# A convolution by Fourier transforms: the last tile's first 13 frequencies go through DRAM, ordered by frequency row, instead of being transposed on chip

## The chip, the cores and the metric

The kernel runs on one NeuronCore of one Trainium2 chip. Its engines are TensorE (PE; its weight loads are listed apart as PEld), VectorE (DVE), ScalarE (ACT), GpSimd (POOL) and SyncE (SP), which here only issues DMAs. The metric is the device time of one execution in microseconds (us); less is better. A profiled execution gives the instructions of each engine with start and duration, the DMA packets, and the TensorE clock that was granted.

## The reference

A 2D circular convolution of one 224 x 224 image with 96 channels by a 7 x 7 kernel with 96 x 96 channels, done by FFT in float32:

```python
"x": (1, 224, 224, 96) bfloat16        "w": (7, 7, 96, 96) bfloat16

wp = jnp.pad(w, ((0, H - K), (0, W - K), (0, 0), (0, 0)))
Xf = rfft2(x.astype(float32), axes=(1, 2))
Wf = rfft2(wp.astype(float32), axes=(0, 1))
Yf = jnp.einsum('bhwi,hwio->bhwo', Xf, Wf)
y = irfft2(Yf, s=(H, W), axes=(1, 2)).astype(bfloat16)
```

## The kernel before

The image's rows are cut into 8 blocks (`NJ`) of 28 output rows (`B`); with the 6 rows of overlap a block has 34 rows (`L`). Along the rows the kernel uses a short transform, along the columns taps. The columns are cut into 7 tiles (`NT`) of 32 columns: 16 pairs (`TW`) of two. The last tile is `TL` = 6.

Per tile there are three stages. **Forward**: matmuls with `Fm` turn the rows of a block into `NS` = 17 frequencies, each with two parts (frequencies 0 and 16 have two real rows each). **Middle**, `b_round(t, s, ...)`, once per tile and frequency: 33 matmuls of 96 columns (22 for frequencies 0 and 16) of the transformed pixels `xf` and their sums `J` with the transformed weights `WF`. A part of the results is copied out of PSUM by ScalarE (`tt_`), VectorE forms `u` and `v`, and the sum `ysum` of the two is the result of one frequency: 128 partitions (16 pairs x 8 blocks, "(w j)") by 384 values (2 parts r, 2 pixels m, 96 channels o). `ysum` runs on VectorE in the rounds in which `b_round` is called with `ydve` true, else on GpSimd after the round's `J` sums. **Inverse**: for a block, 34 values (17 frequencies x 2 parts) become 28 output rows. This needs the frequencies on the partitions, whereas the middle stage leaves the pixels there.

Tiles 0 to 5 turn the data through DRAM: three frequencies at a time (`YGRP`) go into `yf` and from there by one DMA to the scratch tensor `scr`; when a tile is finished, `queue_c` loads it back as `tt` with the frequencies on partitions (pieces of 384 B), and `c_jobs` inverts it during the next tile. The five loads of a tile are `LT`; one of them is made of four DMAs, two of which load 34 partitions each. `pump` issues a load when a buffer is free.

The last tile has no next tile to hide this behind. Before, its results stay on chip: `b_round` writes frequencies 0 to 12 (`SA` = 13) into `YA`, a part of the pixel buffer `xn_all`, and 13 to 16 into `YB`. VectorE turns them in squares of 32 x 32: `turn_a` four times for `YA`, during the rounds 13 to 16, and `turn_b` for `YB` behind the loop. `TA` and `TB` are the turned data. The tail then inverts: `first(j, h)` multiplies `TA` by the matrix `GA` (112 columns: 4 pixel groups x 28 rows; 384 moving columns), `second` adds four matmuls of 96 moving columns for `TB` with `GB`, and evicts the sum to `yo`. There are 16 of these pairs, 8 `first` ahead of the others. Eight output DMAs of 168 KB follow, on SyncE (4), GpSimd (3) and ScalarE (1). `GA` and `GB` come from `G` by `g_parts`: small DMAs to `GX`, then copies to `GY`, done in tiles 3 and 4.

The order of work is written by hand. The instructions of one engine stand in program order. Fills between the two halves of a round (`mid`, `fills`, `pace`) spread the inverse jobs of the tile before: `CQ[t]` = (old, new) tells how many jobs left over from two tiles ago and how many of the last tile's 11 jobs go into tile t; what is left of tile 5's jobs runs behind the loop, before the tail. All DMAs but four of the last ones are issued by SyncE, in program order, each after the semaphores that it waits for.

Line numbers in the profile are of no use here: every instruction goes through the wrapper `_Ordered` and is put down to line 86 (of the kernel before; 87 of the one after). Groups are told apart by the names of their tiles.

Of the kernel before, what the change touches and what calls it, by code (L numbers as in the profile page):

```python
# [8 lines left out]
BF16 = mybir.dt.bfloat16  # L9
F32 = mybir.dt.float32  # L10
# [4 lines left out]
B = 28  # L15
L = B + KT - 1
LC = L - 2
NS = L // 2
# [15 lines left out]
YGRP = ((0, 3), (3, 6), (6, 9), (9, 12), (12, 15), (15, 17))  # L34
SA = 13
NB4 = 4
YMAX = 3
YBUF = 4
JGB = ((0, 3), (3, 6), (6, 9), (9, 12), (12, 15), (15, 17))
LAG = 4  # L40
CQ = {2: (11, 0), 3: (11, 2), 4: (9, 5), 5: (6, 8), 6: (3, 8)}
SH2 = (0, 8, 13, 17)
MERGE = ()
NP2 = 0
# [9 lines left out]
def kernel(  # L54
# [85 lines left out]
    G = cpool.tile([3 * FR, 3 * B], BF16, name="Gm")  # L140
    SR = 32
    SRB = 2 * (NS - SA)
    assert 2 * SA <= SR and NB4 * SRB == SR and 4 * NJ == SR and B <= SR
# [366 lines left out]
    def b_round(t, s, mid, end, ydve=False, planes=()):  # L510
# [5 lines left out]
            1: (Jb[:, 6], Jb[:, 3], Jb[:, 2]),  # L516
            2: (Jb[:, 5], Jb[:, 1], Jb[:, 0]),
        }
        if t == TL:
            yt, i = (YA, 2 * s) if s < SA else (YB, 2 * (s - SA))  # L520
            ym = yt[:, :, i:i + 2, :].rearrange("p g r o -> p g (r o)")
        else:
            for (y0, y1) in YGRP:
                if s == y0:
                    yf_cur[t] = (yf_pool.tile([128, YMAX, 2, 2, C], BF16, name="yf"), y0, y1)
            yf, y0, y1 = yf_cur[t]
            ym = yf[:, s - y0].rearrange("p r m o -> p m r o")

        def conv(bank, col, m, part, add=False, both=False):
# [11 lines left out]
        if s in REAL:  # L541
            for part in range(2):
                conv(b0, part * C, 0, part)
            if t == TL:
                SE.copy(out=tt_.rearrange("p (r m o) -> p r m o", r=2, m=2),
                        in_=b0[:, 0:2 * C].rearrange("p (r o) -> p r o", o=C).unsqueeze(2).to_broadcast([128, 2, 2, C]))
            else:
                SE.copy(out=tt_[:, 0:2 * C], in_=b0[:, 0:2 * C])
            mid()
            for mi, m in enumerate((2, 1)):  # L550
                for part in range(2):
                    conv(b1, (part * 2 + mi if t == TL else mi * 2 + part) * C, m, part)
            if t == TL:
# [10 lines left out]
        else:  # L564
            v = tv_pool.tile([128, 2, 2, C], F32, name="v")
            if merge:
                conv(b0, 2 * C, 0, 0, both=True)
                conv(b0, 2 * C, 2, 0, add=True)
                conv(b0, 3 * C, 1, 0, add=True)
                conv(b0, 0, 0, 1)  # L570
                conv(b0, C, 0, 2)
                SE.mul(out=tt_[:], in_=b0[:, 0:4 * C], mul=-0.5)
                u, pr = tt_[:, 2 * C:4 * C].rearrange("p (m o) -> p m o", m=2), tt_[:, 0:2 * C]
            else:
                for part in range(3):
# [4 lines left out]
                if t == TL:  # L580
# [9 lines left out]
            mid()  # L590
            for mi, m in enumerate((2, 1)):
                for pi, part in enumerate((1, 2)):
                    conv(b1, (pi * 2 + mi if t == TL else mi * 2 + pi) * C, m, part)
            if t == TL:
                VE.tensor_tensor(out=v[:], in0=pr.rearrange("p (r o) -> p r o", r=2).unsqueeze(2).to_broadcast([128, 2, 2, C]),
                                 in1=b1[:, 0:4 * C].rearrange("p (r m o) -> p r m o", r=2, m=2), op=ALU.add)
            else:
                VE.scalar_tensor_tensor(out=v.rearrange("p m r o -> p m (r o)"),
                                        in0=pr.unsqueeze(1).to_broadcast([128, 2, 2 * C]), scalar=-2.0,
                                        in1=b1[:, 0:4 * C].rearrange("p (m q) -> p m q", m=2), op0=ALU.mult, op1=ALU.add)  # L600
            def ysum(eng):
                if t == TL:
# [13 lines left out]
            load["a"] += 490 if merge else 410  # L616
            load["v"] += (560 if ydve else 250 if t < 2 else 0) + (560 if merge else 900)
            end()
        if t != TL and s == y1 - 1:
            dma(scr_tiles[t].rearrange("w j s e -> (w j) s e")[:, y0:y1], yf[:, 0:y1 - y0].rearrange("p s r m o -> p s (r m o)"))  # L620

    scr_tiles = {}
    tt_tiles = {}
# [14 lines left out]
    NA, NBL = C * SR * 2, C * SRB * 2  # L638
    xs = xf_bufs[(TL + 1) % 2].rearrange("c p r s w j -> c (p r s w j)")
    assert NA + 2 * NBL <= 4 * NS * POS * NJ and NA <= 2 * (XW + 32)  # L640
    YA = xn_all[:, 0:NA].rearrange("p (g s o) -> p g s o", s=SR, o=2)
    TA = xs[:, 0:NA].rearrange("p (g w j e) -> p w j g e", j=NJ, w=4, e=4)
    TB = xs[:, NA:NA + NBL].rearrange("p (g w j e) -> p w j g e", j=NJ, w=4, e=4)
    YB = xs[:, NA + NBL:NA + 2 * NBL].rearrange("p (g s o) -> p g s o", s=SRB, o=2)

    def turn(src, dst, g0, g1):
        load["v"] += 120 + 2 * SR * (g1 - g0) / 0.96
        VE.transpose(out=dst.bitcast(F32).rearrange("p (g n k) -> p g k n", n=SR, k=2)[:, g0:g1], in_=src[:, g0:g1])

    def turn_a(i):  # L650
        src = xn_all[:, 0:NA].bitcast(F32).rearrange("p (g k s) -> p g k s", k=2, s=SR)
        turn(src, xs[:, 0:NA], i * C // 8, (i + 1) * C // 8)

    def turn_b():
        load["v"] += 240 + C // NB4 * SR / 0.96
        src = xs[:, NA + NBL:NA + 2 * NBL].bitcast(F32).rearrange("p (g b k s) -> p k g b s", b=NB4, k=2, s=SRB)
        dst = xs[:, NA:NA + NBL].bitcast(F32).rearrange("p (g b j k) -> p k g b j", b=4, j=NJ, k=2)
        for k in range(2):
            VE.transpose(out=dst[:, k], in_=src[:, k])

    def g_parts():
        for q in range(4):
            dma(GX[q * SR:q * SR + 2 * SA, 0, q * B:q * B + B], G[0:2 * SA, 0:B])
            yield
        for q in range(4):
            for b in range(NB4):
# [1 line left out]
                dma(GX[r:r + SRB, 1 + b, q * B:q * B + B], G[2 * SA:2 * NS, 0:B])  # L668
                yield
        for k in range(NB4 + 1):  # L670
            GE.tensor_copy(out=GY[:, k].rearrange("p (m q) -> p q m", q=4), in_=GX[:, k].rearrange("p (q m) -> p q m", q=4))
            yield

    yo_free = [J_bufs[2][0:4 * B, i * PXC * C:(i + 1) * PXC * C] for i in range(2)]
# [120 lines left out]
    for r in range(NS + LAG):  # L795
# [18 lines left out]
        if r == PGRP[-2][1] + 1:  # L814
# [27 lines left out]
    gp = g_parts()  # L842
    for t in range(2, NT):
        if t == TL:
            GE.memset(YA[:, :, 2 * SA:, :].rearrange("p g s o -> p g (s o)"), 0.0)
        else:
            scr_tiles[t] = dr_pool.tile([TW, NJ, NS, 4 * C], BF16, name="scr")
        qs = []
# [14 lines left out]
        for s in range(NS):  # L863
            now = ()
            if s in plan:
                g = plan[s]
                now = jit(t, g + 1) if g + 1 < len(JGB) else jit(t + 1, 0)
            if s == 3:
                queue_c(t - 1)
            if t in (3, 4):  # L870
                next(gp, None)
            mid = fills(qs, 2 * s)
# [17 lines left out]
    MO = 4 * B  # L890

    def first(j, h):
        pc = bank()[0:MO, 0:NC]
        TE.matmul(pc.rearrange("p (w g e) -> p w g e", w=2, e=4), lhsT=GA, rhs=TA[:, 2 * h:2 * h + 2, j], start=True, stop=False)
        return pc

    def second(j, h, pc, yo):
        po = pc.rearrange("p (w g b e) -> p b w g e", w=2, b=NB4, e=4)
        for b in range(NB4):
            TE.matmul(po[:, b], lhsT=GB[:, b], rhs=TB[:, 2 * h:2 * h + 2, j], start=False, stop=b == NB4 - 1)  # L900
        tail_evac(yo[0:MO, (j % 2) * 2 * NC + h * NC:(j % 2) * 2 * NC + (h + 1) * NC], pc, NC)
    order = [(j, h) for j in range(NJ) for h in range(2)]
    warm(WARM0)
    live = {k: first(*k) for k in order[:8]}
# [44 lines left out]
```

## Time and profile before

| | |
|---|---|
| time, median of 3 (range) | 265.35 us (265.25 to 266.07) |
| the profiled execution | 266.41 us, of which the span is 264.70 us |
| PE, DVE, ACT, POOL busy | 252.5, 215.8, 198.6, 101.5 us |
| mean granted TensorE clock | 0.993 |
| DMA | 43.44 MB, mean 164 GB/s; 30,836 of 41,416 packets under 512 B |
| last tile's rounds 13 to 16 on PE | about 244.3 to 250.3 us |
| the tail's first matmul, its last one | 252.78, 259.0 us |

The span is the time from the first to the last instruction; the profiled execution's own time has about 1.7 us more around it. A page of the profile gives busy times, the chain of work that ended last (followed back from the end through what released each step), and groups of instructions with their count, busy time and mean duration. A timeline line has start, duration, engine, operation, tiles (written <- read), count, and in brackets the idle time before it with what ended it. "SPq" is SyncE's sequencer; the duration of its DMA_DIRECT2D is the time to issue, not to move the data. The trace also holds each DMA packet (start, duration, bytes) and each landing, which are counted on a semaphore per DMA. In a table by stretches the columns are PE, PEld, DVE, ACT and POOL busy us (with the number of instructions), the granted clock, the mean DMA busy time in us over the 16 engines, and GB/s.

### The profile page before, as it was taken

Reading aid. Unit: us, or ns where it says so; the run is one execution under the profiler, and the core shown is the slowest. Engines: PE = TensorE matmul, PEld = TensorE weight load, DVE = VectorE, ACT = ScalarE, POOL = GpSimd, SP = SyncE. Lnnn points to the kernel's source line nnn. Section 1 sums busy time; section 2 is a strip of 40 time slices with the busy share of each in tenths; the row PEclk is TensorE's granted clock in tenths of the full one; section 3 lists DMA queues with packets and bytes.
Section 4 is the critical chain, followed back from the end, with each engine's and each line's share of the span. In section 5 each row is a group of like instructions: output and inputs, shape, how many; then the busy total and the mean of one; then the engine's idle time right before and its main releaser. Section 6 shows DMA issues by size and latency. Waiting matters only on the chain.

```text
span 264.7 us, 12207 instructions
## 1 busy us (share of the span) xinstructions
PE 252.5 (95%) x5160; PEld 234.3 (89%) x5160; DVE 215.8 (82%) x459; ACT 198.6 (75%) x500; POOL 101.5 (38%) x166
## 2 busy tenths in 40 slices
PE   8799998999999999999999999999999999999981
PEld 3569898999999999998999998999999999999861
DVE  5729799898978979977888788777978889899981
ACT  5529997659795566898988869989798886666652
POOL 7781033345355553234123332543143222424420
PEclk9999999999999999999999999999999999999997
DMA  6766210451111299896979449597959753585135
GB/s 162 182 192 152 73 51 2 154 159 47 50 47 47 85 254 208 239 268 180 290 226 244 150 108 315 180 258 185 325 193 206 209 186 125 145 169 155 55 111 175
DMA packets 41416, 43.44 MB, mean 164 GB/s; under 512 B 30836, under 2 KB 33104, under 8 KB 41362
## 3 DMA queue, kind: packets, MB, share of 16 engines
q1 hardware_dynamic: 41044, 41.98, 56.6%
q8 instruction: 40, 0.66, 1.1%
q0 software_dynamic: 192, 0.52, 0.7%
q10 hardware_dynamic: 126, 0.17, 0.2%
q14 instruction: 14, 0.11, 0.1%
HBM read 22.09 MB, written 19.66 MB: 158 GB/s over the span
## 4 chain that ended last, share of the span: by engine, by line
PE 82%; ACT 5%; DVE 4%; issue 3%; DMA 3%; POOL 1%; SPq 1%; DVEq 0%; ACTq 0%
PE pb L86 82%; ACT WF L86 3%; DMA WF<-in_x_dram 3%; DVE WF L86 1%; ACT xf L86 1%; POOL yf L86 1%; DVE J L86 1%; DVE u L86 1%; DVE xf L86 1%; SPq L86 1%; DVE yf L86 0%; ACT tt L86 0%; DVE v L86 0%; ACT tt__676 L86 0%; ACT tt__2951 L86 0%
## 5 line engine op out<-in xcount | busy, mean ns | idle before, releaser
L86 PE MATMUL pb<-WF,J 96*128 96x96 bf16 x2821 | 162.6, 206 | 0.5 <-DVE WF L86 0.3
L86 PEld LDWEIGHTS <-J 96*128 96x128 bf16 x2821 | 137.9, 98 | 8.7 <-DVE u L86 1.5
L86 POOL TENSOR_TENSOR yf<-v,u 128x384 bf16<-128x384 f32 x70 | 69.1, 1001 | 129.5 <-issue 69.2
L86 ACT CAST xf<-pb 96x408 bf16<-96x408 f32 (+3 forms) x143 | 67.2, 487 | 10.3 <-PE pb L86 8.5
L86 PE MATMUL pb<-WF,xf 96*128 96x96 bf16 x952 | 60.2, 206 | 1.1 <-ACT xf L86 0.5
L86 DVE TENSOR_TENSOR J<-xf 96x1824 bf16<-96x1824 bf16 (+1 forms) x84 | 57.5, 724 | 0.1
L86 PEld LDWEIGHTS <-xf 96*128 96x128 bf16 x952 | 47.3, 98 | 1.9 <-issue 0.9
L86 PE MATMUL pb<-Fm,xn 118*128 118x136 bf16 (+3 forms) x640 | 45.5, 199 | 0.9 <-DVE u L86 0.8
L86 ACT CAST WF<-pb 96x480 bf16<-96x480 f32 (+1 forms) x59 | 29.0, 573 | 5.0 <-PE pb L86 5.0
L86 PE MATMUL pb<-tt,Gm 102*84 102x384 bf16 (+1 forms) x132 | 32.1, 326 | 0.0
L86 PEld LDWEIGHTS <-xn 118*128 118x128 bf16 x640 | 30.5, 97 | 1.2 <-issue 1.2
L86 ACT CAST yo<-pb 84x384 bf16<-84x384 f32 (+1 forms) x66 | 28.2, 484 | 2.9 <-PE pb L86 2.6
L86 ACT CAST J<-pb 84x384 bf16<-84x384 f32 (+1 forms) x65 | 28.0, 484 | 2.8 <-PE pb L86 2.8
L86 DVE TENSOR_TENSOR J<-J 96x912 bf16<-96x912 bf16 (+2 forms) x42 | 22.8, 542 | 0.0
L86 PE MATMUL pb<-wq 98*128 98x120 bf16 (+1 forms) x288 | 21.2, 225 | 0.0
L86 PEld LDWEIGHTS <-wq 98*128 98x128 bf16 x288 | 19.4, 148 | 0.2
L86 PE MATMUL pb<-wu 128*128 128x512 bf16 x43 | 11.8, 435 | 1.1 <-DVE ct L86 1.1
L86 DVE TENSOR_TENSOR yf<-v,u 128x384 bf16<-128x384 f32 x20 | 11.3, 567 | 0.7
L86 PEld LDWEIGHTS <-Gm 102*84 102x84 bf16 (+1 forms) x132 | 11.1, 117 | 0.8
L86 DVE CAST WF<-pb 96x480 bf16<-96x480 f32 (+1 forms) x13 | 7.5, 610 | 5.4 <-PE pb L86 5.2
L86 POOL TENSOR_TENSOR xn<-v,u 128x384 bf16<-128x384 f32 x8 | 7.2, 926 | 11.8 <-DVE v L86 11.8
L86 ACT COPY xf<-xf 96x816 bf16<-96x816 bf16 (+3 forms) x20 | 11.2, 621 | 0.0
(404 smaller groups left out, 254.3 us busy)
## 6 DMA issues: line engine op xcount, KB each, us to landing
scr<-yf SPq DMA_DIRECT2D x30, 288.0 KB
xn<-in_x_dram SPq DMA_DIRECT2D x12, 672.0 KB
tt<-scr SPq DMA_DIRECT2D x24, 336.0 KB
out_dram<-yo SPq DMA_DIRECT2D x12, 252.0 KB
out_dram<-J SPq DMA_DIRECT2D x12, 252.0 KB
tt<-scr SPq DMA_DIRECT2D x6, 288.0 KB
WF<-in_x_dram SPq DMA_DIRECT2D x2, 672.0 KB
scr<-yf SPq DMA_DIRECT2D x6, 192.0 KB
```

The costliest lines, as they stand in the source:

```text
L86: r = fn(*a, **k)
```

## The change

Frequencies 0 to 12 of the last tile take the way of the other tiles in another order. `b_round` writes them into `yf` like any tile's, and as each group is full a DMA writes it to a DRAM scratch `scra` of 26 rows (13 frequencies x 2 parts) by 128 x 192 values, so that each value row of a frequency is contiguous over all pixels. A group of three frequencies is 288 KB, in pieces of 384 B (192 values); frequency 12 alone is 96 KB. `rows_a` reads them back: each row is split into four (the four pixel groups), which gives 104 partitions of 12 KB, in four pieces of 3 KB each. By `ROWS`, frequencies 0 to 8 (72 partitions) are read at the start of round 11, 9 to 11 (24 partitions) at round 14, and 12 (8 partitions) at round 15; these are places in SyncE's program order, and each read waits for the writes that it reads. The data land in `xn_all` with the frequencies on partitions, so `TA` needs no turn. Only 13 to 16 (`turned`) are turned on chip, by `turn_b` as before.

The other edits: `first` uses 104 partitions instead of 128, and its moving data lie in runs of 192 values instead of 4; `GY` gets 128 columns, the last 16 of which are zeros, for `first` and `second`; PSUM banks are used over 128 partitions, of which 112 are evicted. The sum of frequency 15 goes to VectorE. `queue_c` of tile 5 is called at round 2 of the last tile instead of 3, which puts its loads before the first `scra` write on SyncE. `CQ[6]` is (3, 9) instead of (3, 8), so 2 jobs of tile 5 instead of 3 are left behind the loop. The four transposes `turn_a`, the memset of the unused part of `YA`, and the split of ScalarE's copy in rounds 1 to 12 of the last tile are gone.

```diff
+ROWS = ((0, 9, 11), (9, 12, 14), (12, 13, 15))
-CQ = {2: (11, 0), 3: (11, 2), 4: (9, 5), 5: (6, 8), 6: (3, 8)}
+CQ = {2: (11, 0), 3: (11, 2), 4: (9, 5), 5: (6, 8), 6: (3, 9)}
...
+    KA = 4 * 2 * SA
...
-        if t == TL:
-            yt, i = (YA, 2 * s) if s < SA else (YB, 2 * (s - SA))
-            ym = yt[:, :, i:i + 2, :].rearrange("p g r o -> p g (r o)")
+        turned = t == TL and s >= SA
+        if turned:
+            i = 2 * (s - SA)
+            ym = YB[:, :, i:i + 2, :].rearrange("p g r o -> p g (r o)")
...
-        if t != TL and s == y1 - 1:
-            dma(scr_tiles[t].rearrange("w j s e -> (w j) s e")[:, y0:y1], yf[:, 0:y1 - y0].rearrange("p s r m o -> p s (r m o)"))
+        if not turned and s == y1 - 1:
+            if t == TL:
+                dma(scr_tiles[t].rearrange("a p e -> p a e")[:, 2 * y0:2 * y1], yf[:, 0:y1 - y0].rearrange("p s r m o -> p (s r) (m o)"))
+            else:
+                dma(scr_tiles[t].rearrange("w j s e -> (w j) s e")[:, y0:y1], yf[:, 0:y1 - y0].rearrange("p s r m o -> p s (r m o)"))
...
-    YA = xn_all[:, 0:NA].rearrange("p (g s o) -> p g s o", s=SR, o=2)
-    TA = xs[:, 0:NA].rearrange("p (g w j e) -> p w j g e", j=NJ, w=4, e=4)
+    TA = xn_all[:, 0:NA].rearrange("p (w j e) -> p w j e", j=NJ, w=4)
...
-    def turn_a(i):
-        src = xn_all[:, 0:NA].bitcast(F32).rearrange("p (g k s) -> p g k s", k=2, s=SR)
-        turn(src, xs[:, 0:NA], i * C // 8, (i + 1) * C // 8)
+    def rows_a(s0, s1, split=1):
+        av = scr_tiles[TL].rearrange("a (q p) e -> (a q) (p e)", q=4)[8 * s0:8 * s1]
+        dma(xn_all[8 * s0:8 * s1, 0:NA].rearrange("p (h e) -> p h e", h=split), av.rearrange("p (h e) -> p h e", h=split))
...
-            dma(GX[q * SR:q * SR + 2 * SA, 0, q * B:q * B + B], G[0:2 * SA, 0:B])
+            dma(GX[q:KA:4, 0, q * B:q * B + B], G[0:2 * SA, 0:B])
...
-            GY = g_pool.tile([128, 1 + NB4, 4 * B], BF16, name="GY")
+            GY = g_pool.tile([128, 1 + NB4, 128], BF16, name="GY")
...
+            GE.memset(GY[:, :, 4 * B:], 0.0)
...
-            GE.memset(YA[:, :, 2 * SA:, :].rearrange("p g s o -> p g (s o)"), 0.0)
+            scr_tiles[t] = dr_pool.tile([2 * SA, 128, 2 * C], BF16, name="scra")
...
-            if s == 3:
+            if s == (2 if t == TL else 3):
                 queue_c(t - 1)
+            for r0, r1, ra in ROWS if t == TL else ():
+                if s == ra:
+                    rows_a(r0, r1, 4)
...
-            if t == TL and s >= SA:
-                if s < NS - 1:
-                    now = [lambda i=s - SA: turn_a(i)]
-                else:
-                    mid = lambda m=mid: (m(), turn_a(3))
-            b_round(t, s, mid, fills(qs, 2 * s + 1), bool(now) and not (t == TL and s >= SA), now)
+            b_round(t, s, fills(qs, 2 * s), fills(qs, 2 * s + 1), bool(now) or t == TL and s == NS - 2, now)
...
-        pc = bank()[0:MO, 0:NC]
-        TE.matmul(pc.rearrange("p (w g e) -> p w g e", w=2, e=4), lhsT=GA, rhs=TA[:, 2 * h:2 * h + 2, j], start=True, stop=False)
+        pc = bank()[:, 0:NC]
+        TE.matmul(pc.rearrange("p (w e) -> p w e", w=2), lhsT=GA[0:KA], rhs=TA[0:KA, 2 * h:2 * h + 2, j], start=True, stop=False)
```

More of the change, by code (lines that the diff above doesn't have):

```diff
@@ L142 @@
     SRB = 2 * (NS - SA)
-    assert 2 * SA <= SR and NB4 * SRB == SR and 4 * NJ == SR and B <= SR
+    assert NB4 * SRB == SR and 4 * NJ == SR and B <= SR and any(y0 <= SA <= y1 for y0, y1 in YGRP)
+    KA = 4 * 2 * SA
     XW = 2 * TW * C
@@ L526, in b_round @@
             yf, y0, y1 = yf_cur[t]
+            y1 = min(y1, SA) if t == TL else y1
             ym = yf[:, s - y0].rearrange("p r m o -> p m r o")
@@ L543, in b_round @@
                 conv(b0, part * C, 0, part)
-            if t == TL:
+            if turned:
                 SE.copy(out=tt_.rearrange("p (r m o) -> p r m o", r=2, m=2),
@@ L551, in b_round @@
                 for part in range(2):
-                    conv(b1, (part * 2 + mi if t == TL else mi * 2 + part) * C, m, part)
-            if t == TL:
+                    conv(b1, (part * 2 + mi if turned else mi * 2 + part) * C, m, part)
+            if turned:
                 VE.tensor_tensor(out=yp(ym), in0=pairs(tt_[:]), in1=pairs(b1[:, 0:4 * C]), op=ALU.add)
@@ L579, in b_round @@
                 u = tv_pool.tile([128, 2, C], F32, name="u")
-                if t == TL:
+                if turned:
                     SE.mul(out=tt_[:, 0:C], in_=b0[:, 0:C], mul=-0.5)
@@ L592, in b_round @@
                 for pi, part in enumerate((1, 2)):
-                    conv(b1, (pi * 2 + mi if t == TL else mi * 2 + pi) * C, m, part)
-            if t == TL:
+                    conv(b1, (pi * 2 + mi if turned else mi * 2 + pi) * C, m, part)
+            if turned:
                 VE.tensor_tensor(out=v[:], in0=pr.rearrange("p (r o) -> p r o", r=2).unsqueeze(2).to_broadcast([128, 2, 2, C]),
@@ L601, in ysum @@
             def ysum(eng):
-                if t == TL:
+                if turned:
                     return eng.tensor_tensor(out=yp(ym), in0=pairs(v.rearrange("p r m o -> p (r m o)")),
@@ L636, in load_t @@
                 dma(tt[2 * FR:3 * FR, 4 * j:4 * j + 4], sv[r0 + j * FR:r0 + (j + 1) * FR, 12:16])
-    NA, NBL = C * SR * 2, C * SRB * 2
+    NA, NBL = SR * 2 * C, C * SRB * 2
     xs = xf_bufs[(TL + 1) % 2].rearrange("c p r s w j -> c (p r s w j)")
-    assert NA + 2 * NBL <= 4 * NS * POS * NJ and NA <= 2 * (XW + 32)
-    YA = xn_all[:, 0:NA].rearrange("p (g s o) -> p g s o", s=SR, o=2)
-    TA = xs[:, 0:NA].rearrange("p (g w j e) -> p w j g e", j=NJ, w=4, e=4)
[L643 to L648, printed above, removed]
-    def turn_a(i):
-        src = xn_all[:, 0:NA].bitcast(F32).rearrange("p (g k s) -> p g k s", k=2, s=SR)
-        turn(src, xs[:, 0:NA], i * C // 8, (i + 1) * C // 8)
+    assert 2 * NBL <= 4 * NS * POS * NJ and NA <= 2 * (XW + 32) and KA <= R
+    TA = xn_all[:, 0:NA].rearrange("p (w j e) -> p w j e", j=NJ, w=4)
+    TB = xs[:, 0:NBL].rearrange("p (g w j e) -> p w j g e", j=NJ, w=4, e=4)
+    YB = xs[:, NBL:2 * NBL].rearrange("p (g s o) -> p g s o", s=SRB, o=2)
+    def rows_a(s0, s1, split=1):
+        av = scr_tiles[TL].rearrange("a (q p) e -> (a q) (p e)", q=4)[8 * s0:8 * s1]
+        dma(xn_all[8 * s0:8 * s1, 0:NA].rearrange("p (h e) -> p h e", h=split), av.rearrange("p (h e) -> p h e", h=split))
     def turn_b():
         load["v"] += 240 + C // NB4 * SR / 0.96
-        src = xs[:, NA + NBL:NA + 2 * NBL].bitcast(F32).rearrange("p (g b k s) -> p k g b s", b=NB4, k=2, s=SRB)
-        dst = xs[:, NA:NA + NBL].bitcast(F32).rearrange("p (g b j k) -> p k g b j", b=4, j=NJ, k=2)
+        src = xs[:, NBL:2 * NBL].bitcast(F32).rearrange("p (g b k s) -> p k g b s", b=NB4, k=2, s=SRB)
+        dst = xs[:, 0:NBL].bitcast(F32).rearrange("p (g b j k) -> p k g b j", b=4, j=NJ, k=2)
         for k in range(2):
@@ L670, in g_parts @@
         for k in range(NB4 + 1):
-            GE.tensor_copy(out=GY[:, k].rearrange("p (m q) -> p q m", q=4), in_=GX[:, k].rearrange("p (q m) -> p q m", q=4))
+            GE.tensor_copy(out=GY[:, k, 0:4 * B].rearrange("p (m q) -> p q m", q=4), in_=GX[:, k].rearrange("p (q m) -> p q m", q=4))
             yield
@@ L867 @@
                 now = jit(t, g + 1) if g + 1 < len(JGB) else jit(t + 1, 0)
-            if s == 3:
+            if s == (2 if t == TL else 3):
                 queue_c(t - 1)
+            for r0, r1, ra in ROWS if t == TL else ():
+                if s == ra:
+                    rows_a(r0, r1, 4)
             if t in (3, 4):
                 next(gp, None)
-            mid = fills(qs, 2 * s)
-            if t == TL and s >= SA:
-                if s < NS - 1:
-                    now = [lambda i=s - SA: turn_a(i)]
-                else:
-                    mid = lambda m=mid: (m(), turn_a(3))
-            b_round(t, s, mid, fills(qs, 2 * s + 1), bool(now) and not (t == TL and s >= SA), now)
+            b_round(t, s, fills(qs, 2 * s), fills(qs, 2 * s + 1), bool(now) or t == TL and s == NS - 2, now)
     turn_b()
@@ L900, in second @@
             TE.matmul(po[:, b], lhsT=GB[:, b], rhs=TB[:, 2 * h:2 * h + 2, j], start=False, stop=b == NB4 - 1)
-        tail_evac(yo[0:MO, (j % 2) * 2 * NC + h * NC:(j % 2) * 2 * NC + (h + 1) * NC], pc, NC)
+        tail_evac(yo[0:MO, (j % 2) * 2 * NC + h * NC:(j % 2) * 2 * NC + (h + 1) * NC], pc[0:MO], NC)
     order = [(j, h) for j in range(NJ) for h in range(2)]
```

## The prediction

> **What bounds the kernel now.** I read the page's shares first, then the chain of waits, then the last 40 us by engine and the DMA issues in them.
>
> ```profile
> PE 252.5 (95%) x5160; PEld 234.3 (89%) x5160; DVE 215.8 (82%) x459; ACT 198.6 (75%) x500; POOL 101.5 (38%) x166
> PE 82%; ACT 5%; DVE 4%; issue 3%; DMA 3%; POOL 1%; SPq 1%; DVEq 0%; ACTq 0%
> ```
>
> TensorE is busy 95% of the span and is 82% of the chain. The change adds and removes no matmul, so it can only move TensorE's idle time and the tail behind it. The chain's last pieces (start, length, what) show where idle time is left:
>
> ```profile
> 250.83 1.82 DVE xf L86 x2
> 252.65 0.14 issue
> 252.78 1.49 PE pb L86 x8
> 254.27 4.36 PE pb L86 x64
> 258.66 0.89 ACT tt L86 x2
> ```
>
> TensorE stops at 251.74 (the timeline's two warming matmuls, 251.14 + 0.60) and starts the tail's first 8 matmuls at 252.78, after two transposes (1.82 us from 250.82) and the last sum on VectorE: 1.04 us idle, all that lies open there. The change replaces that gate, call it G = 252.78, by the landing of three readbacks from DRAM. So the DMA queue decides. SyncE's issues in that stretch (start, length of the group):
>
> ```profile
> 228.55 6.69 SPq L86 DMA_DIRECT2D tt<-scr  x7
> 235.34 1.06 SPq L86 DMA_DIRECT2D out_dram<-J  x1
> 236.50 0.32 SPq L86 DMA_DIRECT2D tt<-scr  x1
> 236.91 1.10 SPq L86 DMA_DIRECT2D out_dram<-J  x1
> 239.84 6.18 SPq L86 DMA_DIRECT2D out_dram<-yo  x4
> ```
>
> An issue with room takes 0.32 to 0.35 us (236.50, or 251.40). Here seven take 6.69 us and single ones 1.06 and 1.10: SyncE is held back because the engines have not drained what is queued. The trace's landing records agree: the load issued at 233.10 lands at 239.77, the put issued at 236.91 at 242.33, while an unhindered put (251.40) needs 2.48 us. By stretches (last two columns: DMA busy us, GB/s):
>
> ```profile
> 230.00:232.00 2.00, 2.00 (x46) 1.89 (x43) 1.97 (x4) 1.26 (x5) 0.00 (x0) 1.00 1.10 259
> 232.00:234.00 2.00, 2.00 (x44) 1.88 (x42) 2.00 (x6) 1.53 (x6) 0.55 (x1) 1.00 1.28 209
> 234.00:236.00 2.00, 2.00 (x46) 1.89 (x44) 1.66 (x5) 1.51 (x5) 1.27 (x2) 1.00 0.27 46
> 236.00:238.00 2.00, 2.00 (x46) 1.89 (x44) 2.00 (x5) 1.12 (x4) 0.00 (x0) 1.00 1.02 233
> 238.00:240.00 2.00, 2.00 (x46) 1.89 (x43) 1.69 (x5) 1.30 (x5) 1.50 (x2) 1.00 0.96 269
> 240.00:242.00 2.00, 2.00 (x46) 1.89 (x44) 1.97 (x4) 1.31 (x4) 0.31 (x1) 1.00 0.75 248
> 242.00:244.00 2.00, 2.00 (x46) 1.89 (x44) 2.00 (x6) 0.88 (x5) 0.46 (x1) 1.00 0.04 15
> ```
>
> The queue works without a break from 230 to 242 and is empty only from 242 on. 234 to 236 moves 46 GB/s although SyncE is held: the landing counts show that the two loads of 34 rows use 2 of the 16 engines, and what stands behind them waits. Rows on engines go by the largest divisor up to 16 here (34 rows: 2, 84: 14, 112 and 128: 16), which I carry over: 72 and 24 rows on 12, 8 on 8.
>
> **Part by part.**
>
> *Removed:* four transposes of 128x768 (0.97 + 0.96 + 1.82 us of VectorE), a POOL memset of 1.05 us, and one of two ScalarE copies per round (0.25 + 0.31 us become one of 0.41). TensorE covered all of that but the 1.04 us above; without that cover a transpose shows as the idle time before the tail does now. *Added on VectorE:* the sum of frequency 15 (0.56 us, before 0.93 on POOL). VectorE then ends with v of 15 at 250.90, two sums of 0.56 and 0.51, two transposes of 0.52: 253.0 instead of 254.22. *Moved:* one job of two 384-column matmuls (0.49 us) goes from behind the tile into it; TensorE still ends at 251.74.
>
> *Added on SyncE:* eight DMAs, in this order among those that stay. W0, W1, W2 (frequencies 0-2, 3-5, 6-8; 288 KB each in 768 pieces of 384 B), R0 (72 rows of 12 KB), then tile 5's three puts, W3 (9-11), a put, W4 (12; 256 pieces), R1 (24 rows), a put, R2 (8 rows). R0 waits for W0 to W2, R1 for W3, R2 for W4, and SyncE waits in order: what is queued behind R0 is W3 and W4 themselves.
>
> Price of a W. Writes of 384 B into DRAM are not in the trace. The nearest rows are the 384 B reads: (259 + 209)/2 = 234 GB/s from 230 to 234, so 295 kB in 1.26 us (26 ns a piece and engine). Low end: the reads' best half microsecond, 426 packets, 19 ns a piece, 0.9 us. High end: the longest tenth of the reads' packets, 40 ns, 1.9 us. I take the mean pace of the nearest row, 1.26.
>
> - Tile 5's loads are issued from 228.55 as before (same wait). W0 and W1 come ahead of the put that lands at 242.33: 242.33 + 2 x 1.26 = 244.85. W2's data are there when POOL ends frequency 8 at 240.30, but it queues behind: 246.1.
> - R0 issues at 246.2. First packet 0.6 us later (251.40 to 252.0 in the packet records), 24 pieces per engine x 0.121 us (3 KB packet) = 2.9, start spread 0.4: its engines are free at 250.2. Before, they stood idle in this time (0.04 us busy in 242 to 244).
> - Behind it on the same engines: three puts, 0.74; W3 1.26; a put 0.26; W4 0.42. W3 lands at 252.2 + 0.45 receipt = 252.65, W4 at 253.3.
> - R1 issues at 252.7: 0.6 + 0.4 + 0.97 puts its engines at 254.7. The put between (0.73) and R2 (0.48) follow: 255.9, landing 256.3.
>
> So G moves from 252.78 to 256.3, **+3.5**, with ends +2.1 (19 ns) and +6.3 (40 ns): W0 to W4 stand 4.33 times in the way of R2 (four of 48 pieces, one of 16), so 7 ns less a piece are 208 x 0.007 = 1.5 us, 14 ns more 2.9.
>
> *Clock.* TensorE would now be idle from 251.74 to 256.3, 4.6 us. The granted clock falls after such a stop: TensorE ends at 259.04, and from 261.19 the clock is at half:
>
> ```profile
> 259.04:261.19 2.15, 0.00 (x0) 0.00 (x0) 0.43 (x1) 0.51 (x2) 0.43 (x1) 1.00 0.81 253
> 261.19:263.00 1.81, 0.00 (x0) 0.00 (x0) 0.00 (x0) 0.00 (x0) 0.00 (x0) 0.50 0.68 224
> ```
>
> At the start it becomes full at 5.2, 4.1 us after the first matmul (1.07). A tail that starts cold loses half of up to 4.1 us, 0 to 2.05; I take **+1.5**. [...]
>
> *128 columns.* Weight loads with 112 columns follow each other at (0.70 - 0.13)/11 = 51.6 ns (12 of GY from 254.58), those with 128 columns at (0.95 - 0.10)/20 = 42.6 (21 of J from 248.29). 64 short matmuls x 9 ns = 0.58 us, of which the eviction pair (0.48 on ScalarE, 0.56 on VectorE, 8 each) lets through 0.46 at most and a cold clock less: **-0.2**.
>
> *End.* The last put needs 4.09 us to land because seven before it crowd the engines; the first of them needs 2.81. A slower tail spreads them: **-0.5** (0 to -1.3).
>
> Sum on the profiled execution: 3.5 + 1.5 - 0.2 - 0.5 = **+4.3 us**. That execution took 266.41 us, of it 264.70 span; it is 1.06 over the median of 265.35, and I put the difference on the median: 269.65, say 269.7. The forecast's own range: 2.1 + 0.7 - 0.3 - 0.5 = +2.0 to 6.3 + 2.05 - 0.2 - 0.5 = +7.7, 267.3 to 273.0.
>
> **Rivals.**
>
> 1. *The rows are there in time; faster.* If W0 to W2 slip into the gaps of the queue (234 to 236 moves 46 GB/s, so 14 engines are free there) and cost next to nothing, W2 lands at about 242.9, R0 runs in the empty stretch from 243 to 247, and R2 lands before 251.74. Then the tail starts at 251.74, its short matmuls at max(253.0, 251.74 + 8 x 0.163) = 253.05 instead of 254.27: -1.2, with 128 columns -0.3 more, of which crowded last puts take 0.4 back: 265.35 - 1.1 = 264.2. For it: the stretch 242 to 250 is nearly empty now. Against it: SyncE pushes in order and is held from 231 to 238, so W0 gets no packet into that gap. It decides where a piece costs under some 8 ns, since 208 x 0.018 = 3.7 us then come off G. Chance 0.13.
> 2. *Just in time; no change.* Pieces of 9 to 12 ns put G near 253, 3 us under the forecast's, with an idle stretch too short for the clock to fall, and the wide columns pay the rest back: 265.3. Chance 0.08.
> 3. [...] Chance 0.14. [...]
> 4. *The change does not do what it says* (one column set or row order missing): every part is a plain instruction of a known kind; I give it nothing of its own.
>
> **How the numbers follow.** The forecast has 0.65, the rivals 0.13, 0.08 and 0.14. Within 0.3% (0.8 us, what a measurement of this kernel can tell from no change) lies rival 2; faster is rival 1 (0.13), same 0.08, slower 0.79. The range takes in rival 2 and the forecast's own range and goes a little above it: 265.0 to 274.0. It leaves out rival 1 and about half of rival 3, whose piece may cost less than twice a read.
>
> **What would show it.** TensorE idle before its first tail matmul for 3 us or more with a DMA of xn named as what ended it; R0 issued after 245, W3 after it; the granted clock at 0.5 in part of the tail; GY's weight loads at 42 to 43 ns where the clock is full. I am wrong if R0 is issued before 244, or if a W takes under 0.5 us of the engines' time, or if the first tail matmul starts by 253.

## The result, and the profile after

The changed kernel takes 274.98 us (median of 4 runs, 273.70 to 276.59), the kernel before, beside it, 265.40: a ratio of 1.036, 95% interval 1.034 to 1.039. It is slower by 9.6 us; forecast were +4.3. The profiled execution took 276.02 us, 274.3 of them span, so it is also 9.6 us longer than the profiled execution of before (266.41, span 264.7).

From the page of the changed kernel: the busy shares, the granted TensorE clock in 40 slices of 6.9 us, and the chain by engine.

```profile
PE 253.6 (92%) x5160; PEld 234.3 (85%) x5160; DVE 212.9 (78%) x456; ACT 197.9 (72%) x488; POOL 100.7 (37%) x165
PEclk9999999999999999999999999999999999999577
PE 65%; POOL 7%; issue 7%; DMA 7%; DVE 6%; ACT 4%; SPq 1%; POOLq 0%; DVEq 0%; ACTq 0%
```

TensorE does the same 5160 matmuls in about the same busy time (252.5 before), but its part of the span falls from 95 to 92%, and the clock, which before fell only at 261.19, behind the last matmul, is low in the last three slices. DMA has 7% of the chain instead of 3%. The timeline of TensorE (start, length, what, in brackets the idle time before it and what ended that) shows where:

```profile
249.72 0.60 PE L87 MATMUL pb<-wu 128*128 128x512 bf16 x2
260.75 1.76 PE L87 MATMUL pb<-xn,GY 104*128 104x384 bf16 x5 [10.43 <-DMA xn<-scra]
```

TensorE stops at 250.32 and waits 10.43 us for a read of `scra`; before, it waited 1.05. This execution came to that point 1.42 us earlier than the profiled one of before (251.74), and was already 1.41 us ahead at tile 5's first load (227.14 against 228.55), ahead of all that the change adds to the queue, and 1.37 at its 500th matmul (32.69 against 34.06); so lengths below are counted within one execution. The difference of the spans is then: -1.42 (start of the stretch), +9.38 (idle time, 10.43 less 1.05), +1.06 (the tail's matmuls, 260.75 to 268.07, 7.32 us against 6.26), +0.57 (from the last matmul to the end, 6.23 against 5.66): +9.6.

The chain of waits back from that read (start, length, what):

```profile
239.26 5.39 DMA scra<-yf
244.65 0.02 SPq L87
...
246.55 8.19 DMA scra<-yf
254.75 0.02 issue
254.76 0.30 SPq L87
...
255.57 5.04 DMA xn<-scra
260.61 0.14 issue
260.75 6.14 PE pb L87 x58
```

W2 (239.26) lands at 244.65 and lets R0 go; W3 (246.55) needs 8.19 us to land and holds R1; R2 (255.57) needs 5.04. Between 244.65 and 246.55 SyncE only issues, as its timeline says:

```profile
244.71 0.30 SPq L87 DMA_DIRECT2D xn<-scra  x1
245.06 1.45 SPq L87 DMA_DIRECT2D out_dram<-yo  x3
246.55 0.46 SPq L87 DMA_DIRECT2D scra<-yf  x1
247.11 0.77 SPq L87 DMA_DIRECT2D out_dram<-J  x1
247.92 0.42 SPq L87 DMA_DIRECT2D scra<-yf  x1
254.76 0.30 SPq L87 DMA_DIRECT2D xn<-scra  x1
```

R0 is issued at 244.71, R1 ten microseconds later. What lies between is mostly R0 itself: the trace's landing records have it land at 251.85, 7.14 us after its issue, the three puts issued behind it at 252.23 to 252.65, W3 at 254.75. Not all of this is the reads: fifteen of W3's sixteen landings are in by 253.52, and the last comes 1.23 us after them. The packet records have a load of instructions there, one packet of 16 KB from 252.55 to 253.65; that it held the sixteenth engine fits, but the records name no engine. In three runs below with an R0 of nearly the same length (6.93 to 7.12 us) and no such late landing, R1 is issued 8.56 to 8.72 us after R0, here 10.05. By stretches (engines' busy us; last three columns: granted clock, DMA busy share, GB/s):

```profile
248.00:250.00 2.00, 2.00 (x36) 1.62 (x32) 1.63 (x4) 1.29 (x5) 0.63 (x1) 1.00 0.93 219
250.00:252.00 2.00, 0.32 (x2) 0.00 (x0) 1.25 (x3) 1.05 (x3) 0.00 (x0) 1.00 0.66 193
...
254.00:256.00 2.00, 0.00 (x0) 0.00 (x0) 0.00 (x0) 0.00 (x0) 0.00 (x0) 0.55 0.46 79
...
262.00:264.00 2.00, 2.00 (x15) 1.33 (x14) 0.18 (x1) 0.00 (x0) 0.00 (x0) 0.50 0.00 0
```

The DMA engines are at work when R0 is under way (busy share 0.93 and 0.66 from 248 to 252); it is not a late start. From 254.21 the granted clock is at half, and the first matmuls of the tail run with it.

### The profile page after: what moved, and what is told of

Read it like the earlier page. It is cut to its first block, busy times and chain, and to the rows that moved or that the text cites. A ratio compares the mean times of both kernels' runs of the same rounds, so it can differ in the third digit from the quotient of the medians.

```text
span 274.3 us, 12206 instructions
## 1 busy us (share of the span) xinstructions
PE 253.6 (92%) x5160; PEld 234.3 (85%) x5160; DVE 212.9 (78%) x456; ACT 197.9 (72%) x488; POOL 100.7 (37%) x165
## 4 chain that ended last, share of the span: by engine, by line
PE 65%; POOL 7%; issue 7%; DMA 7%; DVE 6%; ACT 4%; SPq 1%; POOLq 0%; DVEq 0%; ACTq 0%
PE pb L87 65%; POOL ct L87 6%; DMA scra<-yf 5%; ACT WF L87 2%; DMA xn<-scra 2%; DVE WF L87 2%; DVE J L87 2%; POOL yf L87 1%; DVE u L87 1%; DVE v L87 1%; ACT xf L87 1%; SPq L87 1%; DVE yf L87 0%; POOLq L944 0%; DVE tt L87 0%
## 5 line engine op out<-in xcount | busy, mean ns | idle before, releaser
L87 POOL TENSOR_TENSOR yf<-v,u 128x384 bf16<-128x384 f32 x78 | 76.8, 999 | 141.9 <-issue 78.8
L87 PEld LDWEIGHTS <-GY 128*128 128x128 bf16 (+1 forms) x80 | 5.3, 110 | 12.8 <-issue 12.2
L87 PE MATMUL pb<-xn,GY 104*128 104x384 bf16 x16 | 5.3, 423 | 10.4 <-DMA xn<-scra 10.4
L87 DVE CAST tt<-pb 112x384 bf16<-112x384 f32 x8 | 4.3, 555 | 13.0 <-PE pb L87 12.5
L87 DVE TENSOR_TENSOR yf<-v,u 128x384 bf16<-128x384 f32 x24 | 13.6, 565 | 0.8
L87 ACT CAST tt<-pb 112x384 bf16<-112x384 f32 x8 | 3.7, 479 | 13.8 <-PE pb L87 13.7
```

What stands on the lines that cost most here:

```text
L87: r = fn(*a, **k)
```

## The experiments

Fourteen kernels ran, each compared with the kernel before (265.1 to 265.4 us in the median of each set). The ratios below are to it; the changed kernel's is 1.036. Of the edits, the lines that matter are shown; `...` stands for lines left out.

### Is it the readbacks at all: leave them out

```diff
-                if s == ra:
+                if s < 0:
```

> The changed kernel without the three readbacks; it leaves out their data, and the tail multiplies what lies in the pixel buffer. All theories of late rows: TensorE goes from its last warming matmul into the tail (its idle time under 0.3 us), the clock stays full, the short matmuls start with VectorE's transposes about 1.2 us earlier than before the change, 264.2 as in rival 1 of the prediction. If the writes alone disturb the tail (puts held up, evictions waiting for buffers): above 265.4.

Measured: 264.43 us, ratio 0.996 (0.995 to 0.998). The chain's last pieces of this run:

```profile
243.99 10.80 PE pb L87 x178
254.79 0.02 issue
```

TensorE goes through without a stop. All the other parts of the change, the five writes of 384-byte pieces included, cost nothing that shows, and gain the 1 us that the first rival had (264.2). The whole loss is the readbacks and what waits for them. The two last writes, undisturbed here, give the price of a write directly: W3's 768 pieces are done from 245.42 to 246.71 in the packet records, 48 pieces per engine, 26.8 ns each; the forecast had 26.

### Is it the size of the pieces: 3 KB instead of 12 KB

`rows_a` asks for four pieces of 3 KB per row, but both sides of the copy are contiguous, and the trace shows one piece of 12,288 bytes per row. With 16 spare values behind each quarter of a destination row, the pieces stay apart:

```diff
...
+    XP = xn_all[:, 0:TP].rearrange("p (w f) -> p w f", w=4)[:, :, 0:NA // 4]
...
-        dma(xn_all[8 * s0:8 * s1, 0:NA].rearrange("p (h e) -> p h e", h=split), av.rearrange("p (h e) -> p h e", h=split))
+        dma(XP[8 * s0:8 * s1], av.rearrange("p (h e) -> p h e", h=split))
```

> The changed kernel, but the readback's destination has a gap of 16 values after each quarter row, so that a row goes in four pieces of 3 KB instead of one of 12 KB. Theory A (a 12 KB piece is what makes the reads slow: it took 0.46 to 1.67 us in the changed kernel, a 3 KB piece 0.12 us when alone): R0 holds its engines 3 us instead of 5.2, R1 1 instead of 2, so the tail starts 3 to 4 us earlier and the time is about 271. Theory B (the reads are held by something that goes by bytes or by their place in the queue, not by the size of a piece): same start, 275 within 0.8.

Measured: 277.27 us, ratio 1.045 (1.041 to 1.049). R0 now has pieces of 3 KB and takes 7.95 us from issue to landing. The size of the pieces isn't what makes it long; smaller ones are rather worse.

### Is it the order: all writes ahead of the first read

```diff
-ROWS = ((0, 9, 11), (9, 12, 14), (12, 13, 15))
+ROWS = ((0, 9, 13), (9, 12, 14), (12, 13, 15))
```

> The changed kernel with R0 issued at round 13 instead of 11, which puts W3 and W4 ahead of it on SyncE. Theory C (it is the order that costs: W3 and W4 stand behind R0's 5 to 7 us and R1 and R2 behind them): W4 lands by 249, the three reads follow each other from about 247, R2 lands at 255 to 256 instead of 260.6, time 270 to 271. Theory A alone (only the price of the reads): R0 starts 2.5 us later and nothing is won, 275 or more.

Measured: 272.60 us, ratio 1.026 (1.023 to 1.030). Its chain:

```profile
244.98 2.95 DMA scra<-yf
...
248.75 8.80 DMA xn<-scra
```

W3 lands in 2.95 us where it took 8.19 behind R0, so the order's part is real, 2.4 us of the 9.6. But R0 still takes 7.49 us (246.56 to 254.05), R1 and R2 stand behind it, and R2's landing is 8.80 us after its issue: the wait only changes its name.

### Is it tile 5's 34-row loads on two engines

```diff
-                dma(tt[2 * FR:3 * FR, 4 * j:4 * j + 4], sv[r0 + j * FR:r0 + (j + 1) * FR, 12:16])
+                for a, b in ((0, 32), (32, FR)) if t == TL - 1 else ((0, FR),):
+                    dma(tt[2 * FR + a:2 * FR + b, 4 * j:4 * j + 4], sv[r0 + j * FR + a:r0 + j * FR + b, 12:16])
```

> The changed kernel, with the two loads of 34 rows of tile 5 each cut into 32 and 2 rows, so that 16 engines share them instead of 2. Theory D (the backlog on 2 engines holds W0 to W2): W2 lands 2 to 2.4 us earlier, R0 is issued at 242.3 instead of 244.7, the tail starts as much earlier, 272.5 to 273. If the writes of 384 B are the price instead, R0 is issued within 0.5 us of 244.7 and the time is 275 within 0.8.

Measured: 274.12 us, ratio 1.032 (1.027 to 1.037); against the changed kernel the intervals overlap. R0 is issued at 243.91 and takes 7.19 us. This execution is 0.97 us behind the changed kernel's profiled one from its 1000th matmul on, so by the same work R0 is issued 1.8 us earlier, nearly what was expected, and TensorE's wait is 7.44 us instead of 10.43. W2's data exist only when POOL ends frequency 8, at 240.2, so a shorter queue ahead could give little more. Less of it is left at the end: TensorE reached its last warming matmul another 0.6 us late, and the tail's matmuls took 8.34 us instead of 7.32.

### Is it the twelve engines: 64 rows on sixteen

```diff
-ROWS = ((0, 9, 11), (9, 12, 14), (12, 13, 15))
+ROWS = ((0, 8, 11), (8, 12, 14), (12, 13, 15))
```

> The changed kernel with the rows cut at 8, 12 and 13 frequencies instead of 9, 12 and 13: the reads have 64, 32 and 8 rows, so 16, 16 and 8 engines instead of 12, 12 and 8; they still land on neighbouring partitions from 0 up. Theory E (too few engines): R0 holds the queue 12/16 x 64/72 = two thirds as long (4.5 us instead of 6.7 from issue to landing of its data), the tail starts 2 to 3 us earlier, 272 to 273. [...]

Measured: 273.30 us, ratio 1.030 (1.028 to 1.032). R0 has 64 rows on 16 engines, four pieces each instead of six, and takes 6.49 us; it was also issued 1.25 us earlier (243.46). The pieces grow a little as more engines run: 0.90 us on average, 0.86 on 12 engines. 159 GB/s (884,736 bytes from 245.61 to 251.18) become 176 (786,432 bytes from 244.75 to 249.23).

### Is it the source: rows of the input instead of the scratch

Two runs, with the writes and waits kept (lines that are left out make the reads wait for the same writes as before):

```diff
-        av = scr_tiles[TL].rearrange("a (q p) e -> (a q) (p e)", q=4)[8 * s0:8 * s1]
+        av = x.rearrange("a h w c -> (a h w c)").rearrange("(n e) -> n e", e=NA)[8 * s0:8 * s1]
...
```

> All writes W0 to W4 and all waits stay, but the three reads take their 72, 24 and 8 rows of 12 KB from the start of the input x, where they also lie one behind the other (rows 0 to 103 of 12,288 B), and not from the scratch; the rows that the tail computes with are therefore not the frequencies, and the output is not the reference's. Same destination, same engines, same issue order, R0 issued at about 244.7. Theory F (the reads are slow because the rows were written into DRAM a few us before): R0 lands 4 to 5 us after its issue (7.1 in the changed kernel), G at about 258, 272 us. Theory B (the reads are slow because all rows lie side by side in one small stretch of DRAM): 7 us as in the changed kernel, G at 260.7, 275 us. Theory S (the destination or the engines limit them): 7 us too, 275 us.

```diff
+        av = x[0, :, 0:64, :].rearrange("h w c -> h (w c)")[8 * s0:8 * s1]
...
```

> As the run before, but the rows come from x at a stride of 43,008 B (the first 64 pixels of the image rows 0 to 103; 12,288 B each), as the loads of x in other tiles do with half rows, which move 336 GB/s; output again not the reference's. Theory F: R0 takes 4 to 5 us, 272 us. Theory B: 4 to 5 us here, and 7 in the run before. Theory S: 7 us in both, 275 us.

Measured: 275.60 us, ratio 1.039 (1.035 to 1.043), with rows side by side, and 274.29, 1.035 (1.032 to 1.037), with rows 43 KB apart. R0 takes 7.07 and 7.12 us, with a mean of 0.82 us a piece in both. So neither that the rows were just written nor that they lie close together in DRAM makes the read long. The 336 GB/s that the second expectation gives for the kernel's own loads of x is too high for one of them: the six that run one at a time in the trace of before move 123 to 200 GB/s. The timeline of TensorE with rows 43 KB apart:

```profile
259.31 2.72 PE L87 MATMUL pb<-xn,GY 104*128 104x384 bf16 x8 [8.64 <-DMA xn<-in_x_dram]
```

### Is it the bytes: half of each row

```diff
-        dma(xn_all[8 * s0:8 * s1, 0:NA].rearrange("p (h e) -> p h e", h=split), av.rearrange("p (h e) -> p h e", h=split))
+        dma(xn_all[8 * s0:8 * s1, 0:NA // 2], av[:, 0:NA // 2])
```

> All three reads take only the first half of each row, 6 KB instead of 12; the rest of the tail's rows keeps old pixels, so the output is not the reference's. Rows, engines, order, waits and writes stay. If the reads' cost is the time of their bytes on the engines (6 KB packets of x's loads took a mean of 0.34 to 0.43 us), R0 lands 0.9 + 6 x 0.34 to 0.43 + 0.67 = 3.6 to 4.2 us after its issue instead of 7.1, a little under the 4.4 of the forecast, R1 and R2 shorten by some 1 us each, TensorE starts the tail at about 254.5, idle for some 4 us, and the time is 268 to 270: the forecast's 269.7 or a little under. If it is a fixed cost of a read behind writes (issue, waits, receipt), R0 still takes over 6 us and the time stays over 273.

Measured: 270.00 us, ratio 1.019 (1.016 to 1.022). TensorE's wait:

```profile
254.82 2.51 PE L87 MATMUL pb<-xn,GY 104*128 104x384 bf16 x8 [4.47 <-DMA xn<-scra]
```

R0 takes 4.81 us (expected were 3.6 to 4.2), R1 2.59 instead of 3.94, R2 2.86 instead of 5.04. The twelve of R0's pieces that start first take 1.25 us on average, as long as with full rows (1.28); the 60 behind them take 0.34 instead of 0.78. Nothing but the bytes of the three reads was changed, and of the 9.6 us 4.9 are left (270.00 against 265.09). This is also the kernel whose R0 costs nearly what the forecast had put on the full one (4.45), and it runs in what the forecast had said, 269.7.

### Is it the destination's partitions

Three runs spread the rows over more of the 128 partitions. The first also moved `GX` to fit (two DMAs of 32 rows for R0, 64/32/8 rows in all):

```diff
+    SEGS = ((0, 32, 0), (32, 64, 64), (64, 80, 32), (80, 96, 96), (96, 104, 48))
...
+        for i0, i1, p0 in SEGS:
+            if 8 * s0 <= i0 < 8 * s1:
+                dma(xn_all[p0:p0 + i1 - i0, 0:NA], av[i0:i1])
```

> As engines16, but the 64 rows go half to partitions 0 to 31 and half to 64 to 95, the 32 rows half to 32 to 47 and half to 96 to 111, the last 8 to 48 to 55 (the matrix is permuted to match; the arithmetic is the same). [...] Theory E or a limit on the side of DRAM: as engines16, within 0.8 us.

Measured: 276.02 us (274.37 and 277.67), ratio 1.040 (1.035 to 1.045). Two more executions took 279.30 and 279.69; the profiled one is among them. It had a stretch of half clock in the middle, at 168 to 171 us, and came to the tail some 6 us late, so its times say little. The same without the edit of `GX`:

> The scratch is read again, with 64, 32 and 8 rows (16, 16 and 8 engines, as in the run with 64 rows first, 273.3 us), but spread over the partitions: R0 as two DMAs of 32 rows to partitions 0 to 31 and 64 to 95, R1 as two of 16 to 32 to 47 and 96 to 111, R2 to 48 to 55. GX is left as it is, so without the extra DMAs of the disturbed run; the tail multiplies rows of the wrong frequencies, and the output is not the reference's. [...]

Measured: 272.54 us, ratio 1.027 (1.024 to 1.030). R0's first half needs only W0 and W1 and was issued at 242.51, before W2 had landed, which is a second difference; both halves are in 5.87 us after that. The second half was issued 1.71 us after the first, and its pieces begin at about 245.2, when the first half's are nearly done (245.75), so the two groups of partitions were hardly written at the same time. The third run changes the partitions alone:

```diff
+        xr = {0: xn_all[0:128:2], 8: xn_all[1:65:2], 12: xn_all[65:81:2]}[s0]
+        dma(xr[:, 0:NA].rearrange("p (h e) -> p h e", h=split), av.rearrange("p (h e) -> p h e", h=split))
```

> As the run with 64, 32 and 8 rows (16, 16 and 8 engines, 273.3 us, R0 6.49 us from issue to landing, packets of 0.90 us on average), one DMA for each read, same order, but R0's rows go to every second partition from 0 to 126, R1's to 1, 3, ... 63, R2's to 65, 67, ... 79. The tail multiplies rows of the wrong frequencies, so the output is not the reference's. [...]

Measured: 273.89 us, ratio 1.032 (1.030 to 1.035). R0's pieces take 0.72 us on average instead of 0.90, its 64 rows move at 217 GB/s instead of 176 and land after 5.28 us instead of 6.49. But the average hides two parts. The sixteen pieces that start first take 1.30 us (0.95 with the rows in place); the 48 behind them take 0.52 us on average instead of 0.88. At these lengths 16 engines would move 377 GB/s spread and 223 in place (16 x 12,288 bytes over the mean, an estimate). The time is still that of the run with 64 rows in place (273.30): here R0 was issued at 245.23 and not at 243.46, and W3's last landing came 0.9 us after the other fifteen. In the run before, where each half of R0 went to 32 neighbouring partitions, the last sixteen pieces of a half took 0.67 and 0.60 us, between the two. So the spreading shortens the later pieces, with one profile a side; why it does is not settled, the first pieces stay long, and by itself the spreading does not bring the time down.

### The clock, and the wide matrices alone

```diff
-WARM0 = 2
+WARM0 = 48
```

> The changed kernel with 48 instead of 2 warming matmuls before the tail (10 us of TensorE work in the wait for the rows). The clock theory: granted clock full throughout, the first eight tail matmuls 1.3 us instead of 2.7, the tail 1.2 to 1.7 us shorter, time 273 to 274; the rows land as before. If the cold clock costs nothing (evictions or puts set the pace): 275 within 0.8.

Measured: 273.99 us, ratio 1.033 (1.031 to 1.036). TensorE multiplies zeros through the wait, and the granted clock stays full:

```profile
258.00:260.00 2.00, 2.00 (x11) 0.81 (x9) 0.00 (x0) 0.00 (x0) 0.00 (x0) 1.00 0.27 85
260.00:262.00 2.00, 2.00 (x25) 1.48 (x25) 0.28 (x1) 0.11 (x1) 0.00 (x0) 1.00 0.00 0
```

The tail's first 8 matmuls take 1.47 us instead of 2.72, all 80 take 5.67 (260.05 to 265.72) instead of 7.32; the median is 1.0 us below the changed kernel's, with intervals of the ratio that overlap. In the other run the kernel before has only the matrices of 128 columns:

```diff
-            GY = g_pool.tile([128, 1 + NB4, 4 * B], BF16, name="GY")
+            GY = g_pool.tile([128, 1 + NB4, 128], BF16, name="GY")
...
-        pc = bank()[0:MO, 0:NC]
+        pc = bank()[:, 0:NC]
```

> The kernel before with nothing of the change but the tail's matrices of 128 columns. The prediction's term: the tail's short matmuls follow each other at 42.6 instead of 51.6 ns, the tail ends 0.3 to 0.46 us earlier, time 264.9 to 265.1. If the last puts' crowd takes it all: 265.4 within 0.2.

Measured: 265.55 us, ratio 1.001 (1.000 to 1.002).

```profile
251.56 5.82 PE L86 MATMUL pb<-xf,GY 128*128 128x384 bf16 x80 [0.91 <-ACT yo L86]
```

The tail's 80 matmuls take 5.82 us where they took 6.26, as the forecast's price of a weight load says, and the time does not move.

### What helped, put together

All writes first, 64/32/8 rows, the 34-row loads cut, R2 right behind R1 (`ROWS = ((0, 8, 13), (8, 12, 14), (12, 13, 14))`):

> What helped by itself, put together: all writes ahead of the first read, 64/32/8 rows (16, 16 and 8 engines), tile 5's 34-row loads cut in 32 + 2 rows, R2 right behind R1. Measured alone against the changed kernel: -2.4, -1.7 and -0.9 us. If they add, 275.0 - 5.0 = 270.0 us; if they share the same wait (the reads' own 6 to 7 us, which none of them shortens), not under 271. Neither beats the kernel before, 265.4, since the reads cannot be issued before 246.

Measured: 271.17 us, ratio 1.023 (1.020 to 1.025).

```profile
247.83 7.88 DMA xn<-scra
255.71 0.09 issue
255.80 6.91 PE pb L87 x58
```

The three reads, 1.28 MB, stand one behind the other from 245.97 to 255.71, at 179 GB/s while pieces run. The gains share one wait. This is the best full version of the change that ran, and it is 6 us behind the kernel before. Its rows lie in place (its 48 pieces of R0 after the first sixteen take 0.88 us); one with spread rows as well was not run.

## Why the prediction was wrong in size

The direction, the place and the mechanism were right: TensorE idle in front of the tail, a DMA of `xn` named as what ended it, R0 issued and W3 after it, the clock at half, and, without the reads, the first rival's gain. The size was off, for the most part, because of one price.

**The step that failed** is the price of the reads: "24 pieces per engine x 0.121 us (3 KB packet) = 2.9 ... its engines are free at 250.2", and with it R1's "0.97" and R2's "0.48", which use the same packet. The 0.121 us is the median of the 3 KB packets of puts, which go from SBUF to DRAM (their mean is 0.154); R0 goes from DRAM to SBUF. Four of them make 0.48 us for a row of 12 KB. The shortest 12 KB piece in any run takes 0.46, so a row can go at that price, but R0's did not: measured were 0.86 us a row on average, 245.61 to 251.18, 5.57 us. The twelve pieces that start first took 1.28 us, the other 60 took 0.78. The trace of before held transfers of R0's direction, the loads of x: their packets of 6 KB take 0.35 us on average, which makes 4.2 us for six rows, and the six loads that run one at a time, beside other transfers, move their 118 rows at 123 to 200 GB/s, by which R0's 884,736 bytes take 4.4 to 7.2 us. Counted from R0's issue, with the run on half of each row beside it:

| | forecast | changed kernel | half of each row |
|---|---|---|---|
| R0 issue to landing | 4.45 | 7.14 | 4.81 |
| R0 issue to R1 issue (W3 has landed) | 6.5 | 10.05 | 6.73 |
| R1 issue to R2 landing | 3.6 | 5.85 | 3.82 |
| R0 issue to R2 landing | 10.1 | 15.90 | 10.55 |
| time, us | 269.7 | 274.98 | 270.00 |

All but 0.1 of the 5.9 us that the forecast of G was short (+3.5 against +9.38) lie in the reads and in what stands behind them: 15.90 - 10.1 = 5.8. Of these, 2.7 are R0 itself, 2.25 are R1 and R2, and 0.85 lie between R0's landing and R1's issue, where W3's late landing alone has 1.2 us, which the forecast did not have and which is not a price of the reads. The third column, which has no such late landing, shows that the chain of steps was right with another price in it.

The other steps, one by one:

- *W0 to W4 at 26 ns a piece:* right (26.8 ns). The third rival, a write's piece at twice the forecast's price, would have given nearly this time, 269.7 + 208 x 0.026 = 275.1, but it is not the cause: the packets of W3 and W4 take 0.023 us on average in the changed kernel and without the reads, the 384 B packets of before 0.028.
- *R0 issued at 246.2:* in this execution 244.71, with the 1.42 us by which it ran ahead 246.13: right. The forecast's sign, R0 issued after 245, holds only with that shift.
- *72, 24 and 8 rows on 12, 12 and 8 engines:* right by the landing counts. The split in four, by which the step counted 24 pieces per engine, was merged; that was not the cost, as 3 KB pieces show.
- *Clock +1.5 and 128 columns -0.2:* together +1.06 in the tail's matmuls. With wide matrices and a full clock they take 5.82 us in the kernel before, so the clock's part is 7.32 - 5.82 = 1.50, as forecast in this execution, and the columns' part 5.82 - 6.26 = -0.44, near the bound of -0.46; by itself it buys no time. The matmuls kept warm, 5.67, give 1.65. That the size fits so well is partly luck: the clock was at half for 3.70 us of this tail, but in the ten other kernels with an idle TensorE (the disturbed run left aside) for 3.67 to 6.47 us, where the forecast allowed 4.1 at most, and their 80 matmuls took 7.19 to 8.62 us.
- *End -0.5:* wrong in sign in this execution, +0.57. The last put needs 4.59 us to land instead of 4.09. The clock is at half until 264.45, so it slows the first matmuls only: the eight puts are issued within 4.04 us, before within 4.20, so they are spread no further. In eight of those ten kernels the tail is slower (7.84 to 8.62 us) and the end shorter than before's 5.66 (4.92 to 5.53), as the forecast had it. It was not tried by itself.
- *Rival 1, "it decides where a piece costs under some 8 ns":* its time was right for reads that cost nothing; what decided was the reads' price and not the writes'.

What stays open: why the first pieces of a read take 0.95 to 1.30 us, with half of the bytes too (1.25), and how much of the 9.6 us would be left with spread rows. Shown is that the length of the reads goes with their bytes (R0 4.81 us with half of them, 7.14 with all), and not with the source in DRAM (7.07 and 7.12) or a larger piece (7.95 with 3 KB pieces); that the order costs 2.4 us; and, with one profile a side, that spreading the partitions takes the later pieces of R0 from 0.88 to 0.52 us.

## What to carry to other kernels

Price a transfer by whole transfers of the same direction in the trace, from issue to landing, and not by the median of one packet: here a put's packet under-priced a load by almost half, although loads were in the same trace. Look at the partitions on which it lands as well (0.52 us for a later piece on every second partition, 0.88 side by side, in one profile each). Before a detour over DRAM takes the place of work on chip, add up issue to landing of every step of the round trip in series (write, wait, read, and what is queued behind the read), and compare it with the idle time that it can remove: here 16 us from the first read's issue against 1.05 us. And where reads and writes share one in-order queue, a long read also holds the writes that the next read waits for (W3 took 8.19 us to land behind R0, 2.95 ahead of it).

## What the runs showed of the hardware

- Asking for four pieces of 3 KB where both sides are contiguous gave one piece of 12 KB; kept apart, 3 KB pieces made R0 slower (7.95 us against 7.14).
- Reads into SBUF ran at 159 GB/s on 12 engines, 176 on 16, and 217 on 16 with every second partition as destination, where the pieces after the first sixteen took 0.52 us instead of 0.88; the source in DRAM made no difference (7.07 and 7.12 us).
- A read of 8 rows of 12 KB took 5.04 us from issue to landing, with a read of 24 rows and a put ahead of it in the queue; that read of 24 rows, issued when the queue was nearly empty, took 3.94. With half the bytes they took 2.86 and 2.59.
- Writes of 384 B into DRAM cost no more per piece (0.023 us a packet) than reads of that size (0.028).
- One packet of 16 KB that loads instructions (1.10 us, 252.55 to 253.65) stood beside a write whose last landing came 1.23 us after the other fifteen.
